# Selecting v over all 128 rows, last dilated queries in natural order, and a written order from the last unit on, in dilated sliding attention followed by a soft mixture of experts

## The chip, the cores and the metric

The kernel runs on one core of one Trainium2 chip, in one launch. The metric is the device time of a launch in microseconds (us). The kernel before takes 185.99 us, the median of three runs (184.94, 185.99 and 186.16).

## The reference: what is computed

Attention over 8 batches, 8 heads, 576 positions, 64 elements a head. Heads 0 to 3 look at the last 32 positions ("plain"); heads 4 to 7 at every fourth of the last 128 ("dilated"). The result is a matrix `x` of 4608 rows and 512 columns, which goes through a layer of 8 experts with 4 slots each.

```python
    mask_plain = (rel >= 0) & (rel < window)
    mask_dil = (rel >= 0) & (rel < window * dilation) & (rel % dilation == 0)
...
    logits = x @ phi
    d = softmax(logits, over all rows);  slot_input = d.T @ x
    for e in range(E):
        slot_out[e] = relu(slot_input[e] @ w1[e]) @ w2[e]
    return softmax(logits, over the slots) @ slot_out
```

The softmaxes are written short here. No expert can start before the last row of `x` is known, because the slots' inputs are sums over all rows.

## The kernel before

All inputs are fp32 in HBM and become fp16 on the way to SBUF. The DMAs that do this are issued by POOL (GpSimd), in the order in which they are written: for each batch q and k of the plain heads, v of the plain heads, the last 64 rows of v of all heads, q, k and v of the dilated heads (`load_batch`), and then the weights. Each batch has its own 16 KB per partition (`home`), and the weights of expert e go where batch e's inputs were: `load_w1` (L239) and `load_w2` (L250) wait until PE and DVE are done with them. Output DMAs are issued by SP.

The attention works in 32 units `u`, four per batch and two heads each: plain, dilated, plain, dilated. A unit has these steps:

- `transposes` (L261): q and k are turned by PE into PSUM tiles of the pool `ring` (two buffers of one bank) and copied to SBUF by ACT or DVE.
- `scores` (L300): products into tiles of the pool `ps_s` (two buffers of two banks).
- `softmax_parts` (L325): Exp on ACT, then masks on DVE. A dilated head keeps its queries sorted by position mod 4 (class c, 144 each). The first 128 queries of each class go to `P1`, the last 16 to `P2`, where a class's 16 columns stand next to 16 of the zero-padded rest, so that a class has 32 output rows.
- `values` (L367): products with v into `ps_o`, then a reciprocal (L399) and a product (L400) on DVE, which make `x`. For the last dilated queries there are 8 products per head with 32 output rows each, 4 with `P2` and `vd`, 4 with `P2` and the fifth block of `vp`.
- `x_transposes` (L409): `x` is turned into `xT`. For dilated heads ACT copies the first 512 columns and DVE the last 64, both sorting the columns back.

Once per batch, `spread_v` and `select_v` (L198) make the v operands. `select_v` brings the plain heads' v from the loaded form, four rows to a partition, to one row to a partition, by products with `pick`, a matrix of zeros and ones. It works on 32 partitions at a time (L205) into two tiles of `ps_s`, and on the last 64 rows of v in a tile of `ring` (L216 for plain, L225 for dilated heads). ACT copies the tiles to `vp`. A batch's logits, its exponentials and its part of the slots' sums follow some units later (`front_logits`, `front_rows`, `front_slots`). `row_blocks` has 13 blocks, because the last dilated queries stand in classes of 32 rows.

After the last unit, `last_early` (L503) sums the batches before with fp32 products (L509), `last_logits` and `last_slots` add the last batch, and `siT` (L654) is the slots' input. Then for four pairs of experts `expert_in` makes 16 products with `w1` (L675), Relu on ACT (L683), four transposes (L686) and two copies to `hTp` (L691), and `expert_out` makes 8 products with `w2` for each expert (L699). The output stage copies the sums to `so` (L716), multiplies them by the rows' weights `ET` (L735), scales on ACT (L739) and DVE (L741) and writes 12 tiles to HBM (L745, L747).

The order of POOL is written out by hand (`manual_schedule`). On PE, ACT and DVE a planner orders the instructions, by the program's order and its own estimates.

Of the kernel before, what the change touches and what calls it, by code (L numbers as in the profile page):

```python
# [9 lines left out]
FP32 = mybir.dt.float32  # L10
# [5 lines left out]
B = 8  # L16
# [19 lines left out]
CL = S // DIL  # L36
DW = CL + 16
# [6 lines left out]
def constants():  # L44
    j = np.arange(128)[:, None]
    i = np.arange(QW)[None, :]
    d = i - j
    keep = ((d >= 0) & (d < WINDOW)).astype(np.float16)
    m, n = np.arange(128)[:, None], np.arange(64)[None, :]
    ends = (m // 32 == n // 16) & (m % 32 <= n % 16)  # L50
    band = np.concatenate([keep, ends], axis=1).astype(np.float16)
    ident = np.eye(128, dtype=np.float16)
    return band, ident
# [3 lines left out]
def kernel(  # L57
# [17 lines left out]
    mask = consts.tile([128, QW + 2 * N_SLOTS + 256], FP16, name="mask")  # L75
# [7 lines left out]
    nc.sync.dma_start(out=mask[:, 0 : QW + 64], in_=band_dram.ap())  # L83
# [14 lines left out]
    pick = kept([128, 4, 32, 4], "pick")  # L98
    stackI = kept([128, N_SLOTS], "stackI", FP32)
    upper = kept([128, 1], "upper", FP32)  # L100
    phi_by = kept([128, 4, 4, N_SLOTS], "phi_by")
# [10 lines left out]
    nc.vector.memset(phi_by, 0.0)  # L112
# [3 lines left out]
    P2 = kept([128, 2, 4, 2, 32], "P2")  # L116
# [4 lines left out]
    Er = [kept([128, 10, N_SLOTS], f"Er{i}") for i in range(2)]  # L121
# [6 lines left out]
    nc.vector.memset(P2, 0.0)  # L128
    nc.vector.memset(P2[0:1, :, :, 0, 16:32], 1.0)
# [68 lines left out]
    def select_v(b):  # L198
        raw, last = raws[b]["vp"], raws[b]["vt"]
        for i in range(2):  # L200
            sel = ps_s.tile([128, 2, 2, 4, D], FP32, name=f"sel{b}_{i}", tag="s")
            for r in range(4):
                for n in range(2):
                    rows = slice(64 * i + 32 * n, 64 * i + 32 * n + 32)
                    nc.tensor.matmul(  # L205
                        sel[:, n, 0],
                        pick[rows, r].rearrange("p i j -> p (i j)"),
                        raw[rows, :, r, :],
                        start=(r == 0),
                        stop=(r == 3),  # L210
                        tile_position=(64 * i + 32 * n, 0),
                    )
            nc.scalar.copy(out=vp[b % NV][:, 2 * i : 2 * i + 2, :, 0:D], in_=sel[:, :, 0])  # L213
        end = ring.tile([128, 2, 4, D], FP32, name=f"sel{b}_2", tag="ring")
        for r in range(4):
            nc.tensor.matmul(  # L216
                end[:, 0],
                pick[96:112, r].rearrange("p i j -> p (i j)"),
                last[:, 0:4, r, :],
# [3 lines left out]
            )  # L223
        for r in range(4):
            nc.tensor.matmul(  # L225
                end[32 * r : 32 * r + 32, 1],
                ident[96:112, 96:128],
                last[:, 4:8, r, :],
                start=True,
                stop=True,  # L230
                tile_position=(96, 32 * r),
                skip_group_check=True,
            )
# [66 lines left out]
    def scores(u):  # L300
# [3 lines left out]
        for part in range(2):  # L304
# [7 lines left out]
            for at, k0, q0, n in todo:  # L312
                for g in range(2):
                    ks = q0 - 32 * g - 64 * (at // DW) if k0 is None else k0
# [10 lines left out]
    def softmax_parts(u, tiles):  # L325
# [24 lines left out]
        if hp < 2:  # L350
# [8 lines left out]

        nc.vector.tensor_tensor(  # L360
            out=P2.rearrange("p a c s t -> p (a c) s t")[:, :, :, 0:16],
            in0=pr[:, :, :, 128:DW].rearrange("p a c (s t) -> p (a c) s t", s=2),
            in1=mask[:, QW + 64 :].rearrange("p (c s t) -> p c s t", c=8, s=2),
# [3 lines left out]
    def values(u):  # L367
# [7 lines left out]
        for half in range(2):  # L375
# [4 lines left out]
            for i, blk in enumerate(blocks):  # L380
                for h in range(2):
# [7 lines left out]
                    else:  # L389
                        for s in range(2):  # L390
                            for c in range(4):
                                vt = vp[b % NV][:, 5, hl + h] if s else vd[b % 2][:, 4 * (hl + h) + c]
                                mms.append((ot[32 * c : 32 * c + 32, i, h], P2[:, h, c, s], vt))
# [15 lines left out]
    def x_transposes(u):  # L409
# [11 lines left out]
        else:  # L421
            nc.scalar.copy(  # L422
# [3 lines left out]
            nc.vector.tensor_copy(  # L426
                out=xT[:, hp, 512:576].rearrange("c (t k) -> c t k", k=4),
# [353 lines left out]
```

## Time and profile before

| What | Value |
|---|---|
| Time, median of the runs | 185.99 us |
| Span of the profiled execution, first to last instruction | 183.5 us |
| TensorE clock granted, mean | 0.932 |
| PE busy | 151.8 us (83%) |
| DVE, ACT, POOL busy | 117.1, 115.5, 46.9 us |
| Time of the DMA queue of the loads, as a share of 16 engines' span | 93.9% |
| Read from HBM, written to it | 62.02 MB, 9.44 MB |
| `siT` ready | 144.53 us from the span's start |
| First output DMA issued | 158.90 us |

The busy time of PE counts a matmul from its start to its modelled end, and matmuls overlap, so a busy PE is not PE at its peak. A DMA share above 1 means that packets of several transfers were in flight on an engine at once. The page has the span alone; the time of a launch, of which the runs tell, is the span and what lies around it: 185.99 - 183.5 = 2.5 us if the profiled execution was like the median run. All places below are in us from the span's start.

### The profile page before, as it was taken

How to read it: one execution, taken by the hardware profiler on the slowest of the kernel's cores; microseconds unless marked ns; L12 is line 12 of the kernel's file. 1: busy time of each engine (PE TensorE's matmuls, PEld its weight loads, DVE VectorE, ACT ScalarE, POOL GpSimd, SP SyncE). 2: the span in 40 equal slices, each digit the busy share in tenths (PEclk: the TensorE clock that was granted, in tenths of full speed). 3: DMA queues.
4: the chain of work that ended last, by engine and by line, in shares of the span. 5: the costliest groups of instructions: out<-in, count | busy, mean ns of one | idle time of the engine just before them, and what ended most of it. 6: DMA issues, size and time to landing. Idle time of an engine off the chain costs nothing.

```text
span 183.5 us, 6054 instructions
## 1 busy us (share of the span) xinstructions
PE 151.8 (83%) x2595; PEld 105.8 (58%) x2595; DVE 117.1 (64%) x363; ACT 115.5 (63%) x208; POOL 46.9 (26%) x77
## 2 busy tenths in 40 slices
PE   1869999999988989998997998898979998885300
PEld 1637776677676667666765767666768644432000
DVE  7605886388877877878779687786970111496410
ACT  2248845689599789779878959977703022675410
POOL 7752555464554654401102001003100000000000
PEclk9999999999999999999999999999995589998555
DMA  5999999999999999999999999999999995199996
GB/s 103 183 203 203 202 203 201 202 202 204 204 201 201 204 199 204 226 211 221 212 216 216 212 216 216 218 212 218 218 214 220 212 208 105 75 440 427 427 427 262
DMA packets 23978, 41.06 MB, mean 224 GB/s; under 512 B 1680, under 2 KB 20240, under 8 KB 21136
## 3 DMA queue, kind: packets, MB, share of 16 engines
q0 software_dynamic: 21584, 30.79, 93.9%
q1 hardware_dynamic: 2368, 9.89, 13.4%
q8 instruction: 20, 0.33, 0.6%
q14 instruction: 6, 0.05, 0.1%
HBM read 62.02 MB, written 9.44 MB: 389 GB/s over the span
## 4 chain that ended last, share of the span: by engine, by line
DMA 74%; issue 15%; POOL 3%; ACT 2%; DVE 1%; PE 0%; POOLq 0%; DVEq 0%; SPq 0%
DMA home<-in_moe_w_dram 31%; DMA home<-in_v_dram 15%; DMA home<-in_k_dram 12%; DMA home<-in_q_dram 9%; DMA out_dram<-ot 7%; ACT ot L739 2%; DVE ot L741 1%; POOL home L250 1%; POOL home L162 1%; POOL home L239 1%; POOL home L184 0%; POOL home L187 0%; ACT so L716 0%; PE sop L699 0%; PE f L735 0%
## 5 line engine op out<-in xcount | busy, mean ns | idle before, releaser
L400 DVE TENSOR_TENSOR x<-o,rc 128x384 f16<-128x384 f32 x64 | 29.9, 482 | 0.5
L332 ACT ACTIVATE pr<-s 128x960 f16<-128x960 f32 (+1 forms) x32 | 24.7, 780 | 1.8 <-PE s L315 1.8
L344 ACT ACTIVATE pd<-s 128x640 f16<-128x640 f32 x32 | 20.9, 706 | 1.7 <-PE s L315 1.7
L162 POOL DMA_DIRECT2D home<-in_v_dram x24 | 16.6, 692 | 16.6 <-DMA home<-in_k_dram 11.6
L205 PE MATMUL sel<-home,pick 32*128 32x256 f16 x128 | 17.8, 307 | 1.4 <-DMA home<-in_v_dram 1.1
L399 DVE RECIPROCAL rc<-o 128x6 f32<-128x6 f32 x64 | 10.2, 177 | 13.5 <-PE o L395 13.4
L416 PE MATMUL rgx<-ident,x 128*128 128x128 f16 x160 | 15.6, 233 | 3.0 <-ACT qT L295 3.0
L741 DVE TENSOR_SCALAR ot<-f,rrow 128x512 f32<-128x512 f32 (+1 forms) x19 | 12.5, 716 | 7.7 <-DMA out_dram<-ot 5.2
L335 DVE TENSOR_TENSOR Pp<-pr,mask 128x960 f16<-128x960 f16 (+2 forms) x48 | 16.4, 394 | 0.4 <-ACT pr L332 0.4
L280 ACT COPY qT<-rgq 128x576 f16<-128x576 f16 x16 | 10.3, 641 | 9.0 <-PE rgq L275 8.5
L422 ACT COPY xT<-rgx 128x512 f16<-128x512 f16 x16 | 9.6, 601 | 10.0 <-PE rgx L416 10.0
L739 ACT ACTIVATE ot<-f,rrow 128x512 f32<-128x512 f32 (+1 forms) x19 | 11.2, 675 | 7.0 <-DMA out_dram<-ot 6.6
L239 POOL DMA_DIRECT2D home<-in_moe_w_dram x8 | 4.3, 534 | 44.4 <-PE rgq L290 36.5
L213 ACT CAST vp<-sel 128x512 f16<-128x512 f32 x16 | 9.4, 590 | 9.2 <-PE sel L205 9.0
L416 PEld LDWEIGHTS <-x 128*128 128x128 f16 x160 | 10.2, 102 | 7.2 <-issue 5.4
L735 PE MATMUL f<-so,ET 128*128 128x512 f16 (+1 forms) x38 | 11.0, 402 | 3.9 <-ACT ot L739 3.0
L275 PEld LDWEIGHTS <-home 96*64 96x64 f16 x384 | 11.9, 123 | 3.9 <-issue 2.0
L184 POOL DMA_DIRECT2D home<-in_k_dram x16 | 10.6, 661 | 10.1 <-DMA home<-in_q_dram 8.2
L395 PE MATMUL o<-vp,Pp 128*128 128x65 f16 x288 | 12.9, 203 | 0.0
L436 PE MATMUL l<-xT,phi 128*128 128x288 f16 x64 | 10.8, 304 | 2.0 <-ACT qT L280 1.7
L295 DVE COPY kTd<-rgk 128x576 f16<-128x576 f16 x16 | 12.0, 752 | 0.6 <-PE rgk L290 0.5
L295 ACT COPY qT<-rgq 128x576 f16<-128x576 f16 x16 | 10.3, 646 | 3.1 <-PE rgq L290 2.6
(105 smaller groups left out, 292.9 us busy)
## 6 DMA issues: line engine op xcount, KB each, us to landing
home<-in_moe_w_dram POOLq DMA_DIRECT2D x15, 1024.0 KB, 30.1
out_dram<-ot SPq DMA_DIRECT2D x7, 1024.0 KB, 7.5
home<-in_k_dram POOLq DMA_DIRECT2D x16, 288.0 KB, 9.9
home<-in_q_dram POOLq DMA_DIRECT2D x15, 288.0 KB, 9.7
home<-in_v_dram POOLq DMA_DIRECT2D x16, 256.0 KB, 9.8
out_dram<-ot SPq DMA_DIRECT2D x3, 512.0 KB, 6.5
home<-in_moe_w_dram POOLq DMA_DIRECT2D x2, 512.0 KB, 27.3
home<-in_v_dram POOLq DMA_DIRECT2D x8, 64.0 KB, 8.9
```

The lines of the kernel that those rows point to most:

```text
L162: nc.gpsimd.dma_start(out=dst, in_=v[b, h0 : h0 + n_h, r0 : r0 + 4 * n_p, :].rearrange("h (p r) d -> p h (r d)", r=4),)
L205: nc.tensor.matmul(sel[:, n, 0], pick[rows, r].rearrange("p i j -> p (i j)"), raw[rows, :, r, :], start=(r == 0), stop=(r == 3), tile_posi ...
L275: nc.tensor.transpose(rg[64 * h : 64 * h + 64, r, :], raw[:, 2 * hp + h, D * r : D * r + D], ident[0:NP, 0:NP],)
L295: (nc.scalar.copy if nm == "q" else nc.vector.tensor_copy)(out=dst[:, 0:S].rearrange("c (g p a) -> c g p a", g=4, a=3), in_=rg.rearrange(" ...
L332: nc.scalar.activation(out=pr, in_=st[:, :, 0:n], func=AF.Exp, scale=SCALE)
L335: nc.vector.tensor_tensor(out=Pp[:, :, b0 : b0 + nb, 0:w], in0=pr[:, :, at : at + nb * w].rearrange("p h (t c) -> p h t c", c=w), in1=mask ...
L344: nc.scalar.activation(out=pr[:, part].rearrange("p c e t -> p e c t"), in_=st[:, :, 0 : 2 * DW].rearrange("p e (c t) -> p e c t", c=2), f ...
L395: nc.tensor.matmul(to, lhs, rhs, start=(n == 0), stop=(n == len(mms) - 1), skip_group_check=True)
L400: nc.vector.tensor_tensor(out=x[:, blocks[0] : blocks[0] + nb, D * hl : D * hl + 2 * D].rearrange("p t (h d) -> p t h d", h=2), in0=ot[:, ...
L416: nc.tensor.transpose(rg[:, 128 * blk : 128 * blk + 128], x[:, blk, hl : hl + 128], ident)
L739: nc.scalar.activation(out=ot[:, j, d0:d1], in_=fp, func=AF.Copy, scale=scale)
L741: nc.vector.tensor_scalar(out=ot[:, j, d0:d1], in0=fp, scalar1=scale, scalar2=None, op0=ALU.mult)
```

## The change

Three things change. First, `select_v` uses all 128 partitions at once: `pick` has four groups of 132 columns, and a product takes 128 of them from an offset that depends on the row r. The two tiles of the first 512 rows come from `ring` instead of `ps_s`. The last 64 rows of all eight heads are made by four products of 512 columns with `pick_end`. Second, the last 64 dilated queries stand in natural order: the score tails take another range of keys, `P2` gives way to `Pm` (its class's columns 4 apart, 128 wide) and `Pt`, and `values` makes 5 products of 128 output rows per head instead of 8 of 32. The copy of the last 64 columns of `xT` no longer sorts, and it is written ahead of ACT's. `row_blocks` has 9 blocks. Third, from the last unit on PE, DVE and ACT follow a written order, with five extra products into `spare` that nothing reads, and the experts' inputs go one pair ahead of their outputs.

```diff
     def select_v(b):
-            sel = ps_s.tile([128, 2, 2, 4, D], FP32, name=f"sel{b}_{i}", tag="s")
-            for r in range(4):
-                for n in range(2):
-                    rows = slice(64 * i + 32 * n, 64 * i + 32 * n + 32)
+            sel = ring.tile([128, 2, 4, D], FP32, name=f"sel{b}_{i}", tag="ring")
+            for n in range(2):
+                for r in range(4):
                     nc.tensor.matmul(
-                        sel[:, n, 0],
-                        pick[rows, r].rearrange("p i j -> p (i j)"),
-                        raw[rows, :, r, :],
+                        sel[:, n],
+                        pick[:, 2 * i + n, 3 - r : 131 - r],
+                        raw[:, :, r, :],
                         start=(r == 0),
                         stop=(r == 3),
-                        tile_position=(64 * i + 32 * n, 0),
                     )
...
+        end = ring.tile([128, 2, 4, D], FP32, name=f"end{b}", tag="ring")
         for r in range(4):
             nc.tensor.matmul(
-                end[:, 0],
-                pick[96:112, r].rearrange("p i j -> p (i j)"),
-                last[:, 0:4, r, :],
+                end.rearrange("p a h d -> p (a h) d"),
+                pick_end[96:112, 128 * r : 128 * r + 128],
+                last[:, :, r, :],
...
-                    ks = q0 - 32 * g - 64 * (at // DW) if k0 is None else k0
+                    ks = q0 - 64 - TAIL * (2 * (at // DW) + g) if k0 is None else k0
...
+        tails = pr[:, :, :, 128:DW].rearrange("p a c (s t) -> p a c s t", s=2)
         nc.vector.tensor_tensor(
-            out=P2.rearrange("p a c s t -> p (a c) s t")[:, :, :, 0:16],
+            out=Pm.rearrange("p a (c x) -> p (a c) x", c=4)[:, :, 0 : 4 * TAIL : 4],
...
+        nc.vector.tensor_tensor(
+            out=Pt[:, :, 0 : 4 * TAIL].rearrange("p a (t c) -> p a c t", c=4),
...
-                        for s in range(2):
-                            for c in range(4):
-                                vt = vp[b % NV][:, 5, hl + h] if s else vd[b % 2][:, 4 * (hl + h) + c]
-                                mms.append((ot[32 * c : 32 * c + 32, i, h], P2[:, h, c, s], vt))
+                        for c in range(4):
+                            mms.append((ot[:, i, h], Pm[:, h, 128 * c : 128 * c + 128], vd[b % 2][:, 4 * (hl + h) + c]))
+                        mms.append((ot[:, i, h], Pt[:, h], vp[b % NV][:, 5, hl + h]))
...
-    for u in range(NU + 5):
+    for u in range(NU - 1):
...
+    tail = tc.manual_schedule(
+        engines={mybir.EngineType.PE, mybir.EngineType.DVE, mybir.EngineType.Activation}
+    )
+    tail.__enter__()
+    last = ps_s.tile([128, 2, 512], FP32, name="last", tag="s")
+    lr = last_open(last)
+    last_logits(lr, 0)
+    last_logits(lr, 2)
+    values(NU - 1)
+    x_transposes(NU - 2)
+    front_slots(B - 2)
+    spare = ps_s.tile([128, 2, 512], FP32, name="spare", tag="s")
+    last_logits(lr, 1)
+    fill(spare[:, 0], 2)
+    x_transposes(NU - 1)
+    last_sums(last, lr)
+    lps = [ps_o.tile([128, 288], FP32, name=f"l{B - 1}_{c}", tag="o") for c in range(2)]
+    for c in range(2):
+        logits(B - 1, c, lps[c], range(3))
+    last_logits(lr, 3)
+    er = Er[(B - 1) % 2]
+    nc.scalar.activation(out=er, in_=lr[:, 0:9], func=AF.Exp)
+    for c in range(2):
+        logits(B - 1, c, lps[c], (3,))
+        token_weights(B - 1, c, lps[c])
+    fill(spare[:, 0], 1)
+    rtot = last_slots(last, lr)
...
+    fill(spare[:, 1], 2)
+    front_rows(B - 1)
...
+    expert_in(0)
     for pr in range(4):
-        expert_in(pr)
-        if pr >= 1:
-            expert_out(2 * pr - 2)
-            expert_out(2 * pr - 1)
-    expert_out(6)
-    expert_out(7)
+        if pr < 3:
+            expert_in(pr + 1)
+        expert_turn(pr)
+        expert_out(2 * pr)
+        expert_out(2 * pr + 1)
+    tail.__exit__(None, None, None)
```

`expert_turn` has the transposes and the copies to `hTp` that were at the end of `expert_in`. `last_open` opens the sums with a mask (`shut`), `last_sums` has the fp32 products of `last_early`, and `fill(to, n)` is n products of 512 columns:

```python
    def fill(to, n):
        for _ in range(n):
            nc.tensor.matmul(
                to, ident, ET[:, 0:512], start=True, stop=True, skip_group_check=True
            )
```

In the setup, `spread_phi` brings `phi` to one row per partition with 16 small products instead of 4, and the masks of the last dilated queries are loaded in their final form.

## The prediction

> **What bounds the kernel now.** I read the chain of waits first: which work ended last, from the issue of the last weights on.
>
> ```profile
> 112.49 14.40 issue
> ...
> 126.91 0.49 POOL home L239
> ...
> 128.48 28.27 DMA home<-in_moe_w_dram
> 156.74 0.04 issue
> 156.78 0.42 PE sop L699 x4
> 157.21 0.02 issue
> 157.23 0.59 ACT so L716
> ...
> 157.87 0.28 PE f L735
> ...
> 158.18 3.09 ACT ot L739 x6
> 161.27 3.98 DMA out_dram<-ot
> ```
>
> The columns are start, length, what. The second half of the eighth `w2` lands at 156.74; only four products, one copy and the first output tiles stand between it and the output stream. Nothing of the attention is on this chain. Is the landing late because the load was issued late, or because the DMA engines are full? The windows (length, then busy time of PE, PEld, DVE, ACT and POOL, the granted TensorE clock, the DMA share, GB/s) answer that.
>
> ```profile
> 60.00:80.00 20.00, 18.79 (x386) 13.54 (x383) 16.54 (x52) 15.64 (x30) 8.75 (x15) 1.00 1.25 208
> 100.00:110.00 10.00, 9.19 (x173) 6.58 (x169) 8.03 (x26) 7.80 (x16) 0.00 (x0) 1.00 1.03 215
> 150.00:152.00 2.00, 2.00 (x36) 0.97 (x34) 0.26 (x2) 0.18 (x1) 0.00 (x0) 1.00 1.07 215
> ...
> 154.00:156.00 2.00, 1.68 (x31) 0.79 (x27) 0.26 (x2) 0.60 (x1) 0.00 (x0) 1.00 0.31 63
> ...
> 160.00:162.00 2.00, 1.80 (x8) 0.65 (x7) 2.00 (x4) 2.00 (x5) 0.00 (x0) 1.00 1.06 421
> ```
>
> The share is 1 or above from the first loads to 152, then tapers as the 16 engines finish one by one. The last four loads, issued at 126.91, 127.43, 127.95 and 128.48, land 20.0, 24.4, 26.3 and 28.3 us later, at 146.9 (`w1` of expert 7), 151.8 (`w2` of 6), 154.2 and 156.7 (the halves of `w2` of 7): 4.9 us per MB. At 126.91, when POOL's long wait for home 7 ends, some 15 us of older transfers are still queued (`w1` of 6, issued at 111.96, lands 30.1 us later, at 142.1). So loads run at the engines' rate, and the attention would have to be some 15 us later before a queue ran dry. The output stage is likewise full: 9.44 MB at about 427 GB/s are 22.1 us, which is 160.4 to 182.6.
>
> How far behind is the compute? The timeline of PE in the experts' stage:
>
> ```profile
> 145.03 3.17 PE L675 MATMUL h<-home,siT 128*32 128x512 f16 x25
> ...
> 151.35 0.81 PE L699 MATMUL sop<-home,hTp 128*32 128x512 f16 x9
> ...
> 153.06 1.32 PE L675 MATMUL h<-home,siT 128*32 128x512 f16 x16
> 154.00 0.81 PE L699 MATMUL sop<-home,hTp 128*32 128x512 f16 x9
> 155.13 0.41 PE L686 MATMUL tp<-ident,hs 128*128 128x128 f16 x4 [0.32 <-ACT hs L683]
> 155.47 1.72 PE L699 MATMUL sop<-home,hTp 128*32 128x512 f16 x23
> ```
>
> PE arrives at the last four products 0.44 us before their weights (the idle weight-load queue at 156.79 shows it). Compute and loads finish almost together, and the loads decide. Hence the question for every edit: it can gain nothing at the end, and it costs only what exceeds the slack of the compute.
>
> **The change part by part.** POOL's and SP's instruction streams are the same in both kernels, each DMA with the same place and kinds of wait, so the load stream keeps its size and order: 0.
>
> *Selection of v.* Before, per batch: 16 products of 32 rows (L205), 4 of 16 rows (L216), 4 small ones (L225). In the group of lines L205 is 17.8 us busy over 8 batches, 2.2 each; L216 is 4 x 0.108 = 0.43 (four take 0.59, one 0.27), L225 0.2: 2.9 us. After: 16 of 128 rows and 4 of 512 columns. With L216's 0.108 spacing (256 columns) and twice that, 1.73 + 0.86 = 2.6 us: 0.3 less. The other bound: where four L205 stand together, two start 4 ns apart and the next two 0.119 us later, so undisturbed pairs would need 0.95 us, and all of it 1.6; against that the new form loses 1.0 per batch. I take the group's busy time, since only 8 or fewer stand together in the order of before. The Trainium skill ("TensorE: Matmul & The Clock Gate", Part 3: Packing small matmuls) says that matmuls on different row groups run at the same time, which speaks against this edit. The 4 ns agree. By that rule alone it loses the 1.0 us per batch, 8 in all.
>
> Its results move from the scores' PSUM pool to `ring` (two buffers), and `end` waits for ACT's copy of the first `sel` (0.59). The eight products of the second `sel` (0.86) hide it if ACT comes at once; if not, up to 0.6 us per tile, three tiles per batch, with transposes and scores queued behind on PE.
>
> *Last dilated queries.* Each of 16 units trades 16 column-tiled products (about 0.35 us) for ten of full width at 0.03 (L395's spacing): 0.05 less. DVE trades one L360 (0.282) for two of 128 elements; nearest row, L335's 128x128, 0.219: +0.16 per unit, 0.3 per batch, beside some 2 us per batch in which DVE is idle (8.03 of 10 busy). The rows of logits go from 13 to 9 products (0.15 per batch less). Setup adds 12 small products once (0.4), beside the first loads.
>
> Sum for the attention: PE -0.5 per batch, or +0.5 with the pairs' bound; over 7 batches -3.5 to +3.5. I take -1.
>
> *From the last unit on.* Before, the last x is ready at 136.22, but PE is in eight fp32 products (L509, 135.94 to 137.99), so the five transposes start at 137.85; the clock is half from 138 on; `siT` is ready at 144.53. After, the transposes come first: 0.45, ACT's copy 0.59 (covering L509), logits and nine rows 1.0, Exp 0.44, the 45 products of L536 and L542 0.9 at full clock (1.7 measured at half), reciprocal and product 0.65: 4.0 to 4.9, so `siT` at about 140.7. The added `fill` products stand in waits. Gain 3 to 4 us, in slack.
>
> *Experts one pair ahead.* At full clock 16 products of L675 or L699 take 0.94 (153.06 to 154.00). Per pair: 0.94 in, 0.35 turned, 0.35 waiting for DVE's copy of `hTp` (the transposes of its own pair now stand right ahead of it), 0.94 out: 2.6. Four pairs and the first input, less what the last lacks: 10.3 us, against 12.2 measured. From `siT` at 140.7 PE would be done by 151.5 without weights; with them it waits at 146.9, 151.8, 154.2 and 156.74. The attention may be 5 us slower without any effect.
>
> So the finish stays at 156.74 plus 0.42. What is late next is the clock: PE now does only about 20 products of 0.06 between 151 and 156.7. The row that bears on it: the clock was half from 138.0 to 148.2, after a sparse stretch in which PE was 1.3 and 1.5 busy of 2, and again from 168.7. If it is half when the last weights land, L699 takes 0.25 longer (L675 0.63 against 0.38), and the first output products follow at 0.427 instead of 0.216 (L735 after 168.9). The first output DMA leaves about 0.45 later (0.25 and two halves of 0.1 more). Ahead of the fourth stand ten products, 4 x 0.11 + 6 x 0.21 = 1.7 more, of which some 0.5 was waiting for ACT and DVE before: 1.2 later. The stream, 2.45 us per MB against 1.7 for four products, catches that up no more. Bounds 0 to 1.05; I take 0.45, between, as dense work ended the half clock within 3.2 us at 145.
>
> The Trainium skill ("TensorE: Matmul & The Clock Gate", Part 1: The HAM clock gate) says that an idle window of about 3.4 us halves the clock and a busy one restores it; the trace agrees, with 10.2 us of half clock. By that rule the price is the upper bound.
>
> The span goes from 183.5 to about 184.0. The span of one profiled execution lies 2.5 below the median 185.99 of the runs; with the same 2.5, 186.4.
>
> **The rivals.** *Forecast, 0.81:* bound by the last landing, 0 to 1.05 us more from the clock. 185.0 to 187.2, as the runs of before already spread from 184.94 to 186.16.
>
> *Slower by `ring`, 0.11:* the `sel` and `end` tiles each wait for a busy ACT (DVE for the tile before). At 0.6 x 3 per batch and 7 batches, 12.6 us of PE time; less the 4 of the tail, `siT` at 153, 10.3 of experts after it, end of products near 164, 7 us late: 193. It decides from `siT` past 146.4, so from 0.8 us per batch on; at 1.1 it costs 2. For it: PE is the fullest engine (9.19 of 10). Against: in 100 us it waited only 7, and ACT (7.80 of 10) had room.
>
> *Slower by the clock alone, 0.03:* the half clock meets a delay in the first output tiles, 1.9 or more, 188.
>
> *Faster, 0.05:* the timed runs might have PE later than the profile, by a cold stretch before, and the change removes it. The lowest run, 184.94, is a floor for that; over 1% (below 184.1) would need the taper of 152 to 156.4 to shrink by half, which nothing here touches.
>
> **How the numbers follow.** One per cent, 1.86 us, is about what a measurement of this kernel can tell. Faster 0.05, same 0.81, slower 0.11 + 0.03 = 0.14. Likeliest 186.4. The range takes the lowest run less its noise, 184.8, and at the top the clock's full price with some of the `ring` case, 188.0.
>
> **What would show it.** Right: `w2`'s last landing near 156.7 and four products of L699's kind behind it, PE idle over 4 us between 147 and 156, `siT` by 142, DMA share at 1 to 152, a half clock somewhere from 151 to 162. Wrong: a last product more than 1 us behind the last landing; `sel` or `end` with waits above 0.5 us per batch; a landing that moved by more than 1 us; a first output DMA later than 160.

## The result and the profile after

The changed kernel takes 198.79 us, the median of four runs (198.57 to 200.41), against 185.76 us for the kernel before (184.94 to 186.16, four runs). The ratio is 1.0719, with a 95% interval of 1.0664 to 1.0773. The forecast was no change (186.4), so it was wrong by 12.4 us. Ratios in this text leave out runs over 1.5% longer than the shortest of the same kernel, while medians count all, so that a ratio can differ from the quotient of the medians.

The chain of waits of after, from the last batch of the attention on (start, length, what):

```profile
133.17 1.85 PE sel L211 x16
135.02 0.98 PE end L221 x4
136.02 0.60 ACT vp L229
...
158.62 3.32 PE h L687 x25
...
169.35 1.08 PE sop L714 x16
170.45 0.59 ACT so L732
```

Before, this chain ran over the last weights (`DMA home<-in_moe_w_dram`, landing at 156.74). After, no load is on it any more: it runs over the computation of the attention, the tail and the experts. The loads did not get slower, as the DMA row of the page of after shows (40 slices of 4.93 us, busy tenths), and then the windows (columns as before: length, then PE, PEld, DVE, ACT and POOL, granted clock, DMA share, GB/s):

```profile
DMA  5999999999999999999999999999999200099997
```

```profile
100.00:110.00 10.00, 9.51 (x156) 7.21 (x154) 6.15 (x21) 7.62 (x15) 1.06 (x2) 1.00 1.03 215
150.00:152.00 2.00, 1.68 (x8) 1.68 (x8) 0.24 (x1) 0.59 (x1) 0.00 (x0) 0.50 1.07 215
...
160.00:162.00 2.00, 2.00 (x26) 0.60 (x15) 0.00 (x0) 0.60 (x2) 0.00 (x0) 0.61 0.00 0
```

The share is about 1 or above up to 152, and the last load lands at 155.79 (156.74 before), although the last four loads were issued at 136.9 to 138.5 instead of 126.9 to 128.5. Then the DMA engines stand idle until the first output at about 172. In that gap PE works through the experts:

```profile
158.55 3.39 PE L687 MATMUL h<-home,siT 128*32 128x512 f16 x32
161.87 0.41 PE L701 MATMUL tp<-ident,hs 128*128 128x128 f16 x4
162.55 1.05 PE L714 MATMUL sop<-home,hTp 128*32 128x512 f16 x16 [0.27 <-DVE hTp L706]
```

Three places in the traces divide the loss: the end of the last batch's last copy to `vp` (ACT), the end of `siT`, and the start of `so`, the first copy of the output stage. "Batch" is the mean distance from the third batch's last copy to `vp` to the eighth's, divided by five.

| Kernel | batch | last `vp` | `siT` | `so` | time, median |
|---|---|---|---|---|---|
| before | 14.9 | 126.1 | 144.54 | 157.23 | 185.76 |
| after | 16.5 | 136.6 | 157.78 | 170.45 | 198.79 |

So 10.5 us are lost in the attention and 2.7 between there and `siT` (21.2 instead of 18.4); the experts need 12.7 both times. 10.5 + 2.7 = 13.2, and the times differ by 13.0.

What does a batch look like on PE? Here is, of the kernel before, the timeline of PE while a batch's v is selected:

```profile
105.64 0.39 PE L205 MATMUL sel<-home,pick 32*128 32x256 f16 x3
105.96 0.45 PE L416 MATMUL rgx<-ident,x 128*128 128x128 f16 x5
106.34 0.28 PE L205 MATMUL sel<-home,pick 32*128 32x256 f16 x1
```

and after, PE and DVE (the bracket is the idle time ahead and who ended it):

```profile
116.61 1.91 PE L211 MATMUL sel<-home,pick 128*128 128x256 f16 x16
...
118.45 1.03 PE L221 MATMUL end<-home,pick_end 16*128 16x512 f16 x4
...
119.42 0.60 PE L396 MATMUL o<-vp,Pp 128*128 128x65 f16 x14
...
119.93 0.20 DVE L400 RECIPROCAL rc<-o 128x6 f32<-128x6 f32 x1 [1.75 <-PE o L396]
```

Before, the 16 products of the first 512 rows come in pieces of one to four, between transposes and other work; only the eight short ones of the last 64 rows follow the last piece at once (109.43 to 110.4). After, all 20 stand in one piece of 2.8 us. No product of it waits for long (L211 waited 0.2 us in the whole run); it is what stands behind it that waits: the values, and DVE for them, 1.75 us. These values are those of the next batch's first unit, and they read the `vp` that the block has just made.

The theory at this point: the three tiles of `ring` per batch, of a pool with two buffers that the transposes use too, fix the selection's place and shape in PE's order, and that costs the 10.5 us. The rivals: the 128 rows instead of 32, the order of the copies to `xT` (DVE's 64 columns now ahead of ACT's 512), the new last queries, and for the 2.7 us the extra products or the written order.

### The profile page after: what moved, and what is told of

Read it like the earlier page. It is cut to its first block, busy times and chain, and to the rows that moved or that the text cites. A ratio compares the mean times of both kernels' runs of the same rounds, so it can differ in the third digit from the quotient of the medians.

```text
span 197.2 us, 5726 instructions
## 1 busy us (share of the span) xinstructions
PE 159.1 (81%) x2440; PEld 112.0 (57%) x2440; DVE 121.5 (62%) x375; ACT 116.0 (59%) x208; POOL 47.2 (24%) x77
## 3 DMA queue, kind: packets, MB, share of 16 engines
q1 hardware_dynamic: 2368, 9.89, 12.7%
## 4 chain that ended last, share of the span: by engine, by line
PE 46%; DVE 25%; DMA 11%; ACT 9%; issue 3%; POOL 2%; DVEq 0%; ACTq 0%; SPq 0%; POOLq 0%
PE sel L211 8%; DMA out_dram<-ot 6%; DVE x L401 6%; PE l L431 5%; DVE kTd L290 5%; PE o L396 5%; PE s L310 5%; DMA home<-in_v_dram 5%; PE rgx L417 5%; PE end L221 4%; DVE Pp L330 3%; DVE P L348 3%; PE h L687 3%; PE rgq L270 2%; PE sop L714 2%
## 5 line engine op out<-in xcount | busy, mean ns | idle before, releaser
L327 ACT ACTIVATE pr<-s 128x960 f16<-128x960 f32 (+1 forms) x32 | 23.2, 761 | 1.5 <-PE s L310 1.4
L339 ACT ACTIVATE pd<-s 128x640 f16<-128x640 f32 x32 | 22.6, 717 | 0.9 <-PE s L310 0.7
L424 ACT COPY xT<-rgx 128x512 f16<-128x512 f16 x16 | 9.4, 587 | 19.4 <-DVE xT L423 14.5
L169 POOL DMA_DIRECT2D home<-in_v_dram x24 | 16.6, 692 | 15.6 <-DMA home<-in_k_dram 11.2
L330 DVE TENSOR_TENSOR Pp<-pr,mask 128x960 f16<-128x960 f16 (+2 forms) x48 | 17.6, 385 | 4.5 <-ACT pr L327 4.5
L400 DVE RECIPROCAL rc<-o 128x6 f32<-128x6 f32 x64 | 11.1, 179 | 14.0 <-PE o L396 14.0
L417 PE MATMUL rgx<-ident,x 128*128 128x128 f16 x160 | 14.7, 224 | 4.0 <-ACT qT L290 2.5
L211 PE MATMUL sel<-home,pick 128*128 128x256 f16 x128 | 17.1, 291 | 0.2 <-DVE U_sb L500 0.2
L417 PEld LDWEIGHTS <-x 128*128 128x128 f16 x160 | 11.5, 100 | 7.1 <-issue 6.0
L290 ACT COPY qT<-rgq 128x576 f16<-128x576 f16 x16 | 10.3, 643 | 8.8 <-PE rgq L285 8.8
L310 PE MATMUL s<-qT,kTd 64*128 64x144 f16 (+1 forms) x256 | 15.0, 199 | 0.5 <-ACT pr L327 0.4
L421 DVE COPY xT<-rgx 128x576 f16<-128x576 f16 x16 | 7.2, 452 | 12.3 <-PE rgx L417 12.3
L275 ACT COPY qT<-rgq 128x576 f16<-128x576 f16 x16 | 10.3, 643 | 7.3 <-PE rgq L270 7.3
L211 PEld LDWEIGHTS <-pick 128*128 128x128 f16 x128 | 12.7, 104 | 3.2 <-issue 0.6
L191 POOL DMA_DIRECT2D home<-in_k_dram x16 | 10.7, 671 | 10.4 <-DMA home<-in_q_dram 8.2
```

The costliest lines, as they stand in the source:

```text
L169: nc.gpsimd.dma_start(out=dst, in_=v[b, h0 : h0 + n_h, r0 : r0 + 4 * n_p, :].rearrange("h (p r) d -> p h (r d)", r=4),)
L211: nc.tensor.matmul(sel[:, n], pick[:, 2 * i + n, 3 - r : 131 - r], raw[:, :, r, :], start=(r == 0), stop=(r == 3),)
L290: (nc.scalar.copy if nm == "q" else nc.vector.tensor_copy)(out=dst[:, 0:S].rearrange("c (g p a) -> c g p a", g=4, a=3), in_=rg.rearrange(" ...
L310: nc.tensor.matmul(st[:, g, at : at + n], kT[64 * g : 64 * g + 64, ks : ks + 128], qT[64 * g : 64 * g + 64, q0 : q0 + n], start=True, stop ...
L327: nc.scalar.activation(out=pr, in_=st[:, :, 0:n], func=AF.Exp, scale=SCALE)
L330: nc.vector.tensor_tensor(out=Pp[:, :, b0 : b0 + nb, 0:w], in0=pr[:, :, at : at + nb * w].rearrange("p h (t c) -> p h t c", c=w), in1=mask ...
```

## The experiments

Each is compared with runs of the kernel before on the same chip, so the ratios count; the medians of before on the chips used are 185.76 to 186.10, so that a difference of two medians is good to some tenths of a us. Line numbers are those of each kernel. The places in the traces:

| Kernel | batch | last `vp` | `siT` | `so` | time, median |
|---|---|---|---|---|---|
| e_pss | 15.3 | 126.3 | 148.54 | 160.63 | 189.14 |
| e_sel32 | 15.5 | 126.2 | 148.44 | 160.67 | 190.58 |
| e_copy | 17.6 | 141.5 | 161.83 | 172.71 | 201.89 |
| e_nofill | 16.5 | 134.4 | 154.51 | 167.14 | 196.44 |
| b_ring | 17.7 | 147.3 | 165.80 | 177.79 | 204.33 |
| a_split | 15.6 | 130.1 | 150.77 | 163.46 | 192.46 |
| e_oldtail | 16.8 | 138.4 | 156.55 | 167.25 | 195.82 |
| e_pss_oldtail | 15.3 | 124.4 | 144.09 | 156.94 | 185.58 |
| e_pss_oldexp | 15.3 | 126.5 | 148.25 | 161.00 | 189.12 |
| e_pss_nofill | 15.3 | 124.1 | 145.18 | 157.43 | 186.69 |
| e_pss_nofill_early | 15.3 | 124.5 | 143.18 | 156.16 | 185.60 |
| e_pss_copy_nofill_early | 15.6 | 125.8 | 145.58 | 157.94 | 187.17 |

**e_pss: the pool undone.** After, with the two `sel` tiles taken from `ps_s`; still 128 rows.

```diff
-            sel = ring.tile([128, 2, 4, D], FP32, name=f"sel{b}_{i}", tag="ring")
+            sel = ps_s.tile([128, 2, 512], FP32, name=f"sel{b}_{i}", tag="s")[:, :, 0 : 4 * D].rearrange("p n (h d) -> p n h d", h=4)
```

> The changed kernel with one thing undone: the two tiles of the selection of the first 512 rows come from the scores' pool (ps_s) again, still with products over 128 rows. Theory pool (the tiles in ring make the selection one uninterrupted block of 1.85 + 0.98 us per batch that stands on the chain of waits): the planner can put the products in pieces into gaps of PE again, the period of a batch goes from 16.5 to about 15.2 us, the last copy of vp from 136.0 to about 127, and the time from 198.8 to 189 or less. Theory copies (ACT waits for DVE's copy of the last 64 columns of xT, 14.5 us in the trace): period stays within 0.3 of 16.5 us, time above 197. Theory rows (products over 128 rows cost PE more than those of 32): the same, since the rows stay.

Measured: 189.14 us (189.11 to 189.54, four runs), ratio 1.0185 (1.0142 to 1.0228). The pool is worth 9.65 of the 13 us, and the last copy to `vp` comes 10.3 us earlier. On PE the 16 products are in pieces again, one to six at a time.

**e_sel32: the rows undone too.** `sel` in `ps_s`, 32 rows at a time as before (`pick32` is the old `pick`); the last 64 rows as after.

```diff
-                        pick[:, 2 * i + n, 3 - r : 131 - r],
-                        raw[:, :, r, :],
+                        pick32[rows, r].rearrange("p i j -> p (i j)"),
+                        raw[rows, :, r, :],
+                        tile_position=(64 * i + 32 * n, 0),
```

> The changed kernel with the selection of the first 512 rows undone whole: products over 32 rows into tiles of ps_s, as before; the last 64 rows stay with the new form. It has the same order on PE as the run with ps_s tiles and 128 rows, so the difference of the two is the price of the rows alone. Theory pool: within 1% of that run, 189 or less. Theory rows: 4 us or more faster than that run (up to 0.8 per batch). Theory copies: still above 197 in both.

Measured: 190.58 us (188.65 to 194.06), ratio 1.0165 (1.0109 to 1.0221), against 1.0185 of e_pss; `siT` at 148.44 against 148.54. The 128 rows cost and bring nothing that shows.

**e_copy: the order of the copies undone.** After, with ACT's copy to `xT` written ahead of DVE's again. In after, ACT's copy (L424) stood idle 14.5 us behind DVE's.

```diff
-            nc.vector.tensor_copy(out=xT[:, hp, 512:576], in_=rg[:, 512:576])
...
+            nc.vector.tensor_copy(out=xT[:, hp, 512:576], in_=rg[:, 512:576])
```

> The changed kernel with the copies of xT of a dilated unit in the order of before: ACT's 512 columns first, then DVE's 64. Theory copies: ACT's 14.5 us of waiting for DVE go, period from 16.5 to about 15.3 us, time from 198.8 to about 190. Theory pool: the period falls by 0.3 us at most, time above 196.

Measured: 201.89 us (199.38 to 204.24), ratio 1.0780 (1.0698 to 1.0862). It is not the copies: with ACT first a batch takes 17.1 us (17.6 in the table holds 6.8 us of half clock at 81 to 88). ACT's waits for DVE were not what held the batches up.

**e_nofill: the extra products left out.** After, without `spare` and the five products into it, which nothing reads.

```diff
-    fill(spare[:, 0], 2)
...
-    fill(spare[:, 0], 1)
...
-    fill(spare[:, 1], 2)
```

> The changed kernel without the five products into spare that nothing reads. In its trace the clock is half from 144.5 to 161.6 with them, and they take 0.43 us each, two ahead of the last transposes, one ahead of the sums, two ahead of the experts. Theory of the fills as a cost: 1.3 to 2.1 us less, 196.7 to 197.5. Theory of the fills as a cover for the clock: without them the half clock comes earlier or lasts one more stretch of 3.4 us, time 199 to 201.

Measured: 196.44 us (195.65 to 200.11), ratio 1.0556 (1.0498 to 1.0615). The time is 2.35 us less, but in the profiled executions only 1.1 us of that lies behind the last copy to `vp`, where the products stand (21.2 to `siT` in after, 20.1 here). The other 2.2 us are there by the third batch's last copy to `vp` (54.05 and 51.87), where both kernels have the same instructions; after had half clock from 21.6 to 25.0, and e_nofill had none in the attention. The extra products don't keep the clock up in the tail: it is half for 17.1 us with them (144.5 to 161.6) and without them (142.5 to 159.5).

**b_ring: the pool in the kernel before.** The first 512 rows over all 128 rows, into `ring`; all else as before. (The 128 rows come along; e_sel32 found no price for them.)

```diff
-            sel = ps_s.tile([128, 2, 2, 4, D], FP32, name=f"sel{b}_{i}", tag="s")
+            sel = ring.tile([128, 2, 4, D], FP32, name=f"sel{b}_{i}", tag="ring")
...
-                        pick[rows, r].rearrange("p i j -> p (i j)"),
-                        raw[rows, :, r, :],
+                        pick2[:, 2 * i + n, 3 - r : 131 - r],
+                        raw[:, :, r, :],
```

> The kernel before, with one edit: the first 512 rows of v are selected over all 128 rows into two tiles of `ring`, as after; the last 64 rows, the last dilated queries, the tail and the experts stay. If the pool is the cause (three tiles of `ring` per batch instead of one, handed out in the order of the program, so that the products stand as one block on PE): a batch takes 16.2 to 16.6 us instead of 15.0, the last copy to `vp` ends at 134 to 137, `siT` at 153 to 156, and the time is 193 to 196. If the slower batches need the new last queries or the written tail beside the pool: a batch takes at most 15.5 us, the last copy ends before 130 and the time is 185.5 to 187.

Measured: 204.33 us (202.59 to 206.35), ratio 1.0904 (1.0846 to 1.0963). The loss comes with the pool, without the new last queries and the written tail, and it is above the range that was expected. In the profiled execution, which took 206.35 us, three batches take 16.7 us each, the last two 19.6 and 19.1. Windows of these last two:

```profile
117.00:121.00 4.00, 3.39 (x87) 2.59 (x84) 3.62 (x14) 3.26 (x7) 0.00 (x0) 1.00 1.03 215
121.00:131.00 10.00, 9.54 (x76) 6.09 (x76) 4.09 (x10) 3.75 (x7) 0.53 (x1) 0.51 1.03 215
```

The clock was half for 10.2 us in the middle of the attention (and for 3.4 more at 141.6): 76 products in 10 us there, 87 in the 4 us ahead. That explains the last two batches of this execution, the longest of the four; the runs of 202.59 and 202.79 us also lie above the range, and there is no trace of them. The three batches at full clock take 1.8 us each more than before. The first copies to `vp` are late as well: the third batch's last one ends at 58.6, against 51.4 before. On PE the first eight and the second eight products stand 0.1 us apart in b_ring (71.72 to 73.85), with one product of `s` between them and the last 64 rows right behind.

**a_split: the pool kept, the block cut in three.** After, with each of the three tiles written behind another unit of the batch before.

```diff
-        if u % 4 == 3 and u // 4 + 1 < B:
-            spread_v(u // 4 + 1)
-            select_v(u // 4 + 1)
+        if u // 4 + 1 < B and u % 4 > 0:
+            if u % 4 < 3:
+                select_part(u // 4 + 1, (u % 4 - 1,))
+            else:
+                spread_v(u // 4 + 1)
+                select_end(u // 4 + 1)
```

> The kernel after, with the selection of a batch written in three places instead of one: its first tile after the first unit of the batch before, the second after the second, the last 64 rows after the third. All three tiles stay in `ring`, with the same products and copies. If the length of the block on PE is what a batch pays for (16 and 4 products in one piece, with the values behind it): three short pieces bring a batch from 16.5 to 15.3 to 15.8 us and the time to 190 to 193. If each further tile of `ring` costs its place in the queue for two buffers, wherever it stands: a batch stays at 16.3 to 16.7 us and the time at 197 to 200.

Measured: 192.46 us (190.28 to 193.49), ratio 1.0315 (1.0229 to 1.0401), a batch 15.6 us. PE's timeline of a_split:

```profile
104.07 1.03 PE L211 MATMUL sel<-home,pick 128*128 128x256 f16 x8
...
108.69 1.05 PE L211 MATMUL sel<-home,pick 128*128 128x256 f16 x8
...
112.89 1.02 PE L224 MATMUL end<-home,pick_end 16*128 16x512 f16 x4
```

Same tiles, same pool, same products: three pieces of about 1 us instead of one of 2.8, and 6.3 of the 9.65 us are back (by the ratios, 4.0 of the 5.3 per cent). The first piece also stands two units earlier and the second one unit, further from the values that need them, so the run doesn't tell the length of the piece from its place. Five batches in the windows, after first, then a_split:

```profile
54.00:136.60 82.60, 75.44 (x1336) 57.30 (x1334) 61.80 (x190) 62.86 (x116) 14.71 (x25) 1.00 1.10 213
```

```profile
52.20:130.10 77.90, 75.24 (x1339) 55.43 (x1337) 60.39 (x190) 61.90 (x116) 15.52 (x27) 1.00 1.12 212
```

PE is busy for the same 75.2 to 75.4 us in both; its idle time falls from 7.16 to 2.66, which is 0.90 of the 0.94 us per batch. Read with the 1.75 us in which DVE waited, this suggests (no run shows it further) that DVE runs out of work while the long block runs, and that PE later stands idle for what DVE and ACT make. (A busy time runs to the modelled ends, 0.20 us for a group of two products, so shorter gaps count as busy and PE's idle time is a lower bound.)

**e_oldtail: the written tail undone, the pool kept.** After, with the tail and the experts of before, which the planner orders (the diff of the change from the last unit on, taken back).

> The kernel after with `sel` in `ring` and the last queries in natural order, but with the tail and the experts of before, ordered by the planner. If the losses add up (9.7 by the pool, 3.5 by the written tail): the last copy to `vp` ends at 135 to 137, `siT` at 153 to 155 and the time is 194.5 to 196. If the written tail is only late because the pool delays what it waits for: the time stays at 197.5 or more. If the written order is what makes the batches slow: below 190.

Measured: 195.82 us (195.13 to 196.40), ratio 1.0533 (1.0487 to 1.0578): 3.0 us less than after, so in the time the two losses add up. The places came otherwise than expected: the last copy to `vp` ends at 138.4 and `siT` at 156.55, both later than said, and the stage of the experts is 2.0 us shorter (10.7 from `siT` to `so` instead of 12.7), at full clock. The written order is not what makes the batches slow: a batch takes 16.5 us here too (one of 17.9 has 3.4 us of half clock).

**e_pss_oldtail: both undone.** e_pss with the tail and the experts of before. The 128 rows and the natural order of the last queries stay.

> The kernel with the selection in ps_s over 128 rows and the last dilated queries in natural order, but with the planner's order to the end and the experts' order of before (9 row blocks kept). In the run with ps_s tiles the last copy of vp ends at 126.3 (126.1 before), yet the sums' input siT is ready at 148.5 instead of 144.5. Theory tail: those 4 us are the written order's, so siT comes back to 144 to 145.5, the products end within 1 us of the last landing, 185 to 187. Theory masks: they come from the natural order (two masks 0.75 us instead of one of 0.28 on DVE, ACT's copy behind DVE's), so siT stays at 147 or later and the time at 188 or more.

Measured: 185.58 us (184.91 to 187.71, ten runs), ratio 0.9982 (0.9941 to 1.0023). With these two parts back the kernel is where it was, and the last landing decides again (the last load lands at 156.45, `so` starts at 156.94). A batch takes 0.3 us more than before (15.3 against 14.9), which doesn't show in the time; the new last queries may be the reason, but no run undoes them alone.

**e_pss_oldexp: the experts' order undone.** e_pss with `expert_in(pr)` ahead of the outputs of the pair before, written out.

```diff
-    expert_in(0)
     for pr in range(4):
-        if pr < 3:
-            expert_in(pr + 1)
+        expert_in(pr)
         expert_turn(pr)
-        expert_out(2 * pr)
-        expert_out(2 * pr + 1)
+        if pr >= 1:
+            expert_out(2 * pr - 2)
+            expert_out(2 * pr - 1)
+    expert_out(6)
+    expert_out(7)
```

> The kernel with the selection in ps_s and the written order, but in the experts' stage the order of before: the inputs of a pair stand right ahead of the outputs of the pair before, in the written order. Here the loads have all landed before they are needed, so the experts' order alone decides from siT on. In the run with ps_s tiles the stage takes 11.3 us from the first input product to the end of the products, part of it at half clock. Theory of the prediction (one pair ahead costs a wait for hTp of 0.25 to 0.35 per pair, and saves a wait for Relu of 0.3 per pair): within 0.6 us of 189.1. Theory of the change (one pair ahead hides Relu): 1 to 2 us slower, 190 to 191.

Measured: 189.12 us (188.62 to 191.11), ratio 1.0190 (1.0077 to 1.0303), the same as e_pss. The trace says that this is not because the order costs nothing. PE's timeline of e_pss_oldexp:

```profile
148.59 1.10 PE L687 MATMUL h<-home,siT 128*32 128x512 f16 x16
150.44 0.41 PE L701 MATMUL tp<-ident,hs 128*128 128x128 f16 x4 [0.76 <-ACT hs L695]
```

Written in this order PE waits for ACT's `hs`, 0.70 to 0.77 per pair, instead of 0.27 for `hTp`: some 2 us in four pairs. The stage takes 12.4 us (148.59 to `so` at 161.00), all of it at full clock. In e_pss it takes 11.3 (149.31 to 160.63), although its first 32 products ran at half clock for the most part (2.8 us instead of 1.9), so some 10.4 at full clock. Half clock lasted 6.8 us in the tail of e_pss_oldexp and 13.7 in that of e_pss, and in these two executions that makes up for most of the 2 us; the other runs have no trace.

**e_pss_nofill and e_pss_nofill_early: what in the written tail costs.** e_pss without the five products; and this with the last unit's values and the transposes before them ahead of `last_logits(lr, 2)`, which waits for ACT's copy to `xT`.

```diff
     last_logits(lr, 0)
-    last_logits(lr, 2)
     values(NU - 1)
     x_transposes(NU - 2)
+    last_logits(lr, 2)
```

> The kernel after with the `sel` tiles in `ps_s` and without the five products into `spare`; the values of the last unit stay behind `last_logits(2)`. It stands between the version with both (189.1) and the one with neither and the values moved ahead (185.6). If the five products are most of the loss in the tail: `siT` at 145 to 146.5 instead of 148.5, 186.3 to 187.3. If the place of the values is most of it: `siT` at 147 or later, 188 to 189.

> The kernel with the selection in ps_s, with two edits in the written order: the five products into spare are left out, and the products of the last unit's values stand ahead of the second group of last_logits, which waited for ACT's copy of xT (0.50 us on PE, with a clock that then fell). Theory tail: 2.3 us from the five products (0.43 each at half clock, 1.83 of them on the chain in the run with ps_s tiles), about 1 us from the values: 185.5 to 187, bound by the landing. Theory masks: 1.5 to 2.3 us at most, 187 or more.

Measured: 186.69 us (185.93 to 187.57, nine runs; ratio 1.0044, 1.0016 to 1.0072) and 185.60 us (184.63 to 187.16; ratio 0.9992, 0.9956 to 1.0029). From e_pss on, the products are 2.45 us and the place of the values 1.1. But in the profiled executions only 1.1 of the 2.45 lie behind the last copy to `vp` (22.2 and 21.1 to `siT`); the rest came earlier, though PE's instructions up to the last unit are the same: e_pss had 6.8 us of half clock at 35, in a batch of 18.7 us that takes 15.8 in e_pss_nofill. The next 2.5 (21.1 to 18.6) came with the values' place, and part of them may be the clock, which is half from 140.0 for 6.8 us there, from 135.4 for 13.7 in e_pss_nofill. Of the 2.5, 1.1 show in the time, because then the last landing decides again. PE's timeline of e_pss in the tail:

```profile
135.42 0.27 PE L476 MATMUL e<-quarter,ET 128*128 128x1 f16 x4 [1.75 <-DVE Er L474]
136.18 0.43 PE L458 MATMUL last<-phi,xT 128*128 128x32 f16 x9 [0.50 <-ACT xT L424]
...
138.89 1.01 PE L561 MATMUL spare<-ET,ident 128*128 128x512 f16 x2
139.70 0.74 PE L417 MATMUL rgx<-ident,x 128*128 128x128 f16 x5
```

The values come right behind these 2.25 us of waiting, and the transposes of the last `x` (ready at 138.18) start only at 139.70, behind a group of `last_logits` and two of the extra products. Moved ahead, in e_pss_nofill_early:

```profile
132.38 0.57 PE L396 MATMUL o<-vd,P 128*128 128x65 f16 x8 [0.49 <-DVE P L348]
...
137.13 2.03 PE L516 MATMUL last<-stackI,U_sb 128*128 128x32 f32 x8
139.00 0.90 PE L431 MATMUL l<-xT,phi 128*128 128x288 f16 x6
```

and the chain of waits of that kernel ends with the last weights, as before:

```profile
126.95 28.71 DMA home<-in_moe_w_dram
...
155.71 0.42 PE sop L710 x4
```

**e_pss_copy_nofill_early: ACT's copy first on top of that.** The edit of e_copy in e_pss_nofill_early.

> As the run without the five products and with the last values earlier, and with ACT's copy of 512 columns of xT ahead of DVE's 64 again. With the tiles in ring this order was no faster (199 to 204 against 198.8), though ACT waited for DVE 14.5 us in the changed kernel. Theory copies: ACT's wait for DVE (8.8 us in 100 with ps_s tiles) sits on the chain of the tail at least, 0.5 to 1 us earlier siT than the run without this edit. Theory slack: siT within 0.5 us, time the same, because the landing decides.

Measured: 187.17 us (185.23 to 187.95), ratio 1.0051 (1.0009 to 1.0092). Again no gain: `siT` comes 2.4 us later (145.58 against 143.18), which neither theory had. No version that was run beats the kernel before: where the compute is out of the way, the last landing stands at 155.7 to 156.7.

## Why the prediction was wrong

**The step that failed** is the attention's sum, "I take -1" for a range of -3.5 to +3.5, and in it the term for the move to `ring`, "up to 0.6 us per tile", which was left out of the sum and kept as a rival at 0.11. It was priced as waits of PE for a copy. PE waited 0.2 us for the products of `sel` in the whole run. What the move did is to turn many small pieces between other work into one block of 2.8 us with the values behind it. Against e_pss that cost 1.2 us per batch (16.5 and 15.3) from the third on, whose last copy was 4.0 later already: 10.3 in all. Three pairs of kernels differ in the pool alone; their medians differ as follows: after and e_pss by 9.65 us, e_nofill and e_pss_nofill by 9.75, e_oldtail and e_pss_oldtail by 10.24. With b_ring (the loss in the kernel before) they put it on the pool; a_split puts two thirds to three quarters of it on the length of the block and its place right ahead of the values that need it. That the block comes from two buffers handed out in the program's order is argued from how the pool is used; what was shown is the block and its price. The rival had the right place. Its size (0.6 x 3 over 7 batches, 12.6) is near by luck, since the waits that it adds up did not occur, and "ACT had room" was no argument against it, because ACT's room is not what it took. The sum has a slip besides: with the pairs' bound it is +1.0 less 0.25, so +0.75 per batch and 5.3 over 7, not 3.5; that changes nothing of the above.

**The loads: right.** They were issued 10 us later and landed 0.9 us earlier, with the share at 1 to 152, as the 15 us of queued transfers promised.

**The selection's own size: right.** 20 products take 1.85 + 0.98 us per batch where 2.6 were worked out. The bound from pairs of 32-row products, 1.0 us per batch, did not come: a batch takes 14.7 to 16.0 us in e_sel32 and 14.8 to 15.9 in e_pss. By the rule of the Trainium skill ("TensorE: Matmul & The Clock Gate", Part 3: Packing small matmuls), that matmuls on different row groups run at the same time, e_sel32 should have been the faster by that much. Its products do start in pairs 3 to 4 ns apart, in pieces of one to six between other work, but neither the batches nor the times show the gain.

**The last queries: no harm, but a term mis-sized.** The two masks take 0.455 and 0.508 us where 0.219 each was taken from a product with as many elements. They overlap (`Pt` starts 0.24 after `Pm`), so that DVE's busy time rises from 11.9 to 12.4 us per batch (0.3 was worked out). It may be the 0.3 us per batch of e_pss_oldtail, which the loads hide; that was not shown.

**The tail: wrong sign.** `siT` was to come 4.0 to 4.9 us after the last `x`, a gain of 3 to 4; it came 10.4 after it, 8.3 before, and 8.1 in the best version. Three terms failed. The `fill` products don't "stand in waits": they hold up the transposes and `siT` (1.1 us). The fp32 products weren't covered by ACT's copy: they start after a wait for `sixes` and last until 139.0 in e_pss_nofill_early, while the copy was done at 137.15, so that the logits wait 1.85 us for PE. And the clock was half, which the sum left out: the 40 products of L541 take 1.38 us, where 0.9 was taken for these and five more. The place of the values behind `last_logits(lr, 2)` wasn't priced at all (1.1 us of time).

**The experts: right for the new order, wrong for the gain.** A pair takes 2.57 us (2.6 worked out). The whole stage took 11.85 (158.55 to 170.4), of which the first 32 products at half clock are 1.5 more than their 1.9 at full clock, so 10.35 at full clock, as forecast (10.3). But the 12.2 us of before held half clock too: in e_oldtail, where the clock was full, the old order took 10.6 (156.67 to `so` at 167.25). Against the planner's version of the old order, in which other products run while ACT makes `hs` (PE waits 0.17 to 0.32 for it in e_oldtail), the new one is worth some 0.2 us, not 1.9. Against the old order written out (e_pss_oldexp, 12.4 us) it is worth 2.0.

**The slack of 5 us: wrong,** because it was made of the two gains that didn't come. With `siT` at 145.18 (e_pss_nofill), 0.64 later than before, the time is already 0.44% above before.

**The signs that were named** did what they should in part: the last product 15 us behind the landing, the first output after 160 and `siT` past 146.4 told of the failure. "`sel` or `end` with waits above 0.5 us per batch" did not occur, and would have cleared the pool of the blame.

What stays open: why the clock fell in the attention of some kernels and not of others. e_pss, e_pss_oldexp and e_sel32 have their last copy to `vp` at 126.2 to 126.5 and the kernels without the extra products and with `ps_s` at 124.1 to 125.8; each of the first three had a half-clock stretch there (6.8 us at 35, 6.8 at 34, 3.4 at 80), each of the others one of 3.4 us at 16 to 17, and no run tells why. Nor was it settled why the clock fell in the middle of b_ring. And DVE's wait of 1.75 us behind the block is one row, not the whole price: in e_pss, too, DVE waits for `o` between 55 and 121 (6.7 us in 4 waits, 7.6 in 8 in after), so how the 1.2 us per batch divide over the engines was not taken further than the idle time of PE in a_split. Nor was it asked where the loss ahead of the third batch comes from: most of it is there at the first batch's last copy to `vp` (18.5 in e_nofill, 15.7 in e_pss_nofill).

## What to carry to other kernels

A tile moved to another pool is a change of order: compare the order of instructions before and after, and price the longest piece that now stands together, by who waits behind it, not by whether its own instructions wait. Two versions with the same time can differ by 2 us in a stage when their clocks differ: compare the stage and its clock before a cost is called nothing. A saving measured in a stage at half clock must be worked out again at full clock before it is called slack. And products that only keep an engine busy belong where nothing queues behind them; here they cost time and kept no clock up.

## What the runs showed of the hardware

The half-clock stretches that end within the span had lengths of 3.4, 6.8, 10.2, 13.7 and 17.1 us, multiples of 3.4, and PE's busy time did not tell when one begins or ends. After, from 144.50 to 161.60:

```profile
144.50:161.60 17.10, 15.45 (x177) 10.33 (x176) 3.87 (x13) 2.78 (x6) 0.00 (x0) 0.50 0.58 119
```

PE counts as busy for 15.45 of 17.10 us there, and from 151.40 to 154.80 for all of 3.40. The Trainium skill ("TensorE: Matmul & The Clock Gate", Part 1: The HAM clock gate) has a window of about 3.4 us, and full clock after one that is busy; the lengths agree with that window, but if the trace's busy time is what counts, the clock should have come back by 154.8. It came back at 161.6, 3.0 us into the experts' 32 dense products. With the idle window that the prediction names for the fall, the trace of before agrees in the length alone (10.2 us): ahead of the fall at 138.0, PE was busy for 2.87 of the last 3.40 us and 2.53 of the 3.40 before them, and its longest idle time was 0.87.

Two DVE products with 128x128 results in fp16 took 0.455 and 0.508 us, where L335 of before took 0.219 for as many elements. Both new ones write their 16-element runs with a step of four elements; that this is the reason was not tried.

The eight fp32 products of the sums took the same at either clock: 2.03 us at full clock (L516 of e_pss_nofill_early, from 137.13), 2.04 at half (L516 of after, from 150.77). The 32 fp16 products of L687 took 3.39 us in after, at half clock for most of it, where 1.9 is their time at full clock.
